# A new order for the last 138 steps of a written-out schedule: gated linear attention followed by a hard-swish feed-forward block

## The chip, the cores and the metric

The kernel runs on one core of a Trainium2 chip. The metric is the device time of one execution in microseconds (us), the median of several runs. The profile is one further execution taken by the hardware profiler; it gives every instruction's start and duration, counted from the start of the span.

Five engines work side by side, each with its own stream of instructions in a fixed order: TensorE (PE, matrix products; PEld is its weight load), VectorE (DVE), ScalarE (ACT), GpSimd (POOL) and SyncE (SP), which here issues all the transfers to and from device memory.

## The reference

Two blocks run one after the other. The first is a recurrent attention, per batch and head, over 768 time steps with a 48 x 48 state:

```python
for t in range(S):
    state = alpha[:, :, t, :, None] * state + np.einsum('bhd,bhe->bhde', k[:, :, t], v[:, :, t])
    y[:, :, t] = np.einsum('bhd,bhde->bhe', q[:, :, t], state)
```

Its output is laid out as 3072 tokens by 384 features and goes through a feed-forward block with 2048 hidden features:

```python
h = x @ w_in
g = h * np.clip(h + 3.0, 0.0, 6.0) / 6.0
return g @ w_out
```

## The kernel before, in words

**Tiling.** The attention works on chunks of 128 tokens (numbered 0 to 23, six for each of four batches). Two chunks make a group of 256 tokens (numbered 0 to 11), and the feed-forward block runs once per group. For groups from 2 on, both matrix products of that block are done by recombined blocks (fewer products, at the price of sums before and after them): sums of input blocks on VectorE, 20 products for the first matrix, seven for the second, and sums of the results.

**How the order is set.** Nothing is scheduled by a planner at build time. The kernel holds a text of 1,788 short words at the end of the main function (L763 on); `run` splits it and calls one small function for each word. A word is a step name with its numbers, such as `P.11.6` for product 6 of group 11. Within an engine, instructions run exactly in the order of the words; between engines, semaphores hold an instruction back until what it reads is written and what it overwrites has been read.

**The steps that matter here**, with the lines of the profile:

- `xc.g.i` (L537, L539; VectorE, 128x128): one of eleven sums of input blocks.
- `M.g.i` (L600; TensorE): one of 20 first products, four matmuls of 128x128; those that begin an accumulation name one of the four PSUM banks.
- `n.g.i.z` (L606; ScalarE): copies a product out of PSUM into slot z, one of sixteen areas of 128x512.
- `o.g.o.step` (L537, L539, L541; VectorE, 128x512): combines products into hidden block o (0 to 7).
- `e.g.o.z` (L494; ScalarE) and `h.g.o` (L498; VectorE): the hard-swish gate of that block; z is one of two buffers between them.
- `s.g.i` (L647, L664; VectorE): six sums of the gated hidden blocks for the second matrix.
- `P.g.i` (L703; TensorE): one of the seven second products, eight matmuls with 192 columns. The first four of them read the first half of the operand and the last four the second half.
- `K.g.i` (L682; ScalarE): keeps an intermediate result of these products.
- `G.g.i.z` (L719 on VectorE for i of 0 to 2, L716 on ScalarE for i = 3): forms one quarter of the group's output (128x192) in output buffer z, one of four; `G.g.0` follows product 1, `G.g.1` product 4, `G.g.2` product 5 and `G.g.3` product 6.
- `O.g.i` (L724; issued on SyncE): stores that quarter to device memory, 96 KB. Before buffer z is written again, its store must have landed.

Group 11 is the last one. Its seventh product, `P.11.6`, is the last work of TensorE; `G.11.3` then copies the result and `O.11.3` stores it. After the last step, SyncE waits for all stores and the engines meet in a closing exchange of semaphores (it carries line L928).

The last two lines of the text of steps, as they were:

```python
e.11.2.0 h.11.2 s.11.4 e.11.3.1 h.11.3 P.11.1.0 s.11.5 G.11.0.1 O.11.0 O.10.3 K.11.1
P.11.4 G.11.1.2 P.11.5 G.11.2.1 O.11.2 P.11.6 G.11.3.0 O.11.3 O.9.2 O.11.1
```

Of the kernel before, what the change touches and what calls it, by code (L numbers as in the profile page):

```python
# [17 lines left out]
def kernel(  # L18
# [42 lines left out]
    G = 2  # L61
# [510 lines left out]
    for i in range(8):  # L572
        r, o = divmod(i, 3)
        spots.append(raws[r].rearrange("p n w -> p (n w)").bitcast(FP)[:, o * QB : (o + 1) * QB])
    xc = consts.tile([C, len(X_SUMS), C], FP, tag="xc")
# [174 lines left out]
    with tc.manual_schedule():  # L750
# [133 lines left out]
               M.10.12 M.10.5 e.10.1.0 sv.23.1 n.10.12.13 qa.23.0 n.10.5.15 o.10.3.0 M.10.6.1  # L884
               o.10.3.1 M.10.13 n.10.13.13 o.10.2.0 e.10.3.1 M.10.18.3 n.10.18.13 o.10.2.1 o.10.6.0
               ya.22.1 yb.22 ya.23.2 yb.23 cy.23 M.10.15.0 M.10.16 M.10.14 M.10.19 cy.22 o.10.7.0
               h.10.1 xc.11.1 xc.11.3 o.10.4.0 xc.11.0 M.10.17 xc.11.4 o.10.6.1 xc.11.5 xc.11.6
               e.10.2.0 h.10.2 M.11.0.1 xc.11.2 P.10.0.2 xc.11.8 o.10.7.1 n.11.0.13 e.10.7.0 xc.11.7
               M.11.7.0 o.10.5.0 h.10.3 xc.11.9 h.10.7 e.10.6.1 e.10.5.0 h.10.5 M.11.1 K.10.0
               n.11.7.14 n.11.1.9 e.10.4.0 P.10.1.3 O.9.0 M.11.8 M.11.2 n.11.2.15 h.10.4 h.10.6  # L890
               G.10.0.2 s.10.0.10 xc.11.10 s.10.2.8 s.10.1.12 P.10.3.3 K.10.2 s.10.3.11 s.10.5
               s.10.4 M.11.3 M.11.4 n.11.4.10 P.10.2 o.11.0.0 e.11.0.0 M.11.9 o.11.1.0 M.11.5 K.10.1
               P.10.4 G.10.1.0 O.10.1 h.11.0 e.11.1.1 h.11.1 n.11.5.12 M.11.10 M.11.15.1 n.11.10.8
               P.10.5 G.10.2.0 O.10.2 O.9.1 O.10.0 M.11.11 n.11.11.11 M.11.16 o.11.4.0 M.11.18.3
               n.11.18.10 o.11.7.0 o.11.6.0 M.11.12 n.11.12.15 o.11.3.0 M.11.17 M.11.19 o.11.5.0
               M.11.13 o.11.7.1 e.11.4.0 h.11.4 n.11.13.10 o.11.2.0 e.11.7.1 P.10.6 h.11.7 G.10.3.0
               M.11.14 o.11.6.1 e.11.5.0 e.11.6.1 M.11.6.3 P.11.0.1 h.11.5 h.11.6 s.11.0.15
               s.11.1.14 s.11.3.10 P.11.3.2 K.11.0 s.11.2.11 o.11.2.1 o.11.3.1 P.11.2 K.11.2
               e.11.2.0 h.11.2 s.11.4 e.11.3.1 h.11.3 P.11.1.0 s.11.5 G.11.0.1 O.11.0 O.10.3 K.11.1
               P.11.4 G.11.1.2 P.11.5 G.11.2.1 O.11.2 P.11.6 G.11.3.0 O.11.3 O.9.2 O.11.1""")  # L900


# [30 lines left out]
```

## Time and profile before

| what | value |
|---|---|
| median of 3 runs | 536.4 us (536.31 to 536.47) |
| the profiled execution's own time | 536.33 us |
| its span, first to last instruction | 534.5 us |
| TensorE busy | 524.2 us, 98% |
| VectorE busy | 477.1 us, 89% |
| ScalarE busy | 257.6 us, 48% |
| GpSimd busy | 50.4 us, 9% |
| transfers | 43.0% of 16 engines' span |
| granted TensorE clock | full, in all 40 slices |

The time of the profiled execution is 1.8 us above its span: that lies around the instructions, outside what the profile shows. A busy share is an average over the whole span; what a changed order does has to be read where it stands, in the last eighth of the span and in what comes after TensorE's last product.

### The profile page before, as it was taken

The page shows a single profiled execution, that of the slowest core. Times are in us where ns is not written, and L with a number is a line of the kernel's source. Part 1 is how long each engine was busy: PE and PEld are TensorE (multiplying, and loading weights), DVE is VectorE, ACT ScalarE, POOL GpSimd, SP SyncE. Part 2 cuts the span into 40 slices and gives each one's busy share as a digit, 9 for nine tenths or more (in the row PEclk, how much of TensorE's full clock was granted, in tenths as well). Part 3 has the DMA queues.
Part 4 walks back from the last instruction along what each step waited for, and adds up shares of the span by engine and source line. Part 5 has one row for each costly group of instructions (what it writes and reads, how often), then busy time and mean ns, then how long its engine had stood idle before and what let it go on. Part 6 is the DMA issues. An engine that isn't in the chain of part 4 may idle for free.

```text
span 534.5 us, 15145 instructions
## 1 busy us (share of the span) xinstructions
PE 524.2 (98%) x6306; PEld 498.9 (93%) x6306; DVE 477.1 (89%) x849; ACT 257.6 (48%) x503; POOL 50.4 (9%) x71
## 2 busy tenths in 40 slices
PE   7799999999999999999999999999999999999997
PEld 7698886789999999999999999999999999999996
DVE  6999989999999899998999999999999898586381
ACT  3889864212653553543644434642633544553330
POOL 5333435100000000000010000000000000000000
PEclk9999999999999999999999999999999999999999
DMA  9998877006615155254354455055364042100001
GB/s 174 215 255 256 208 220 164 7 2 158 149 32 121 28 132 130 50 136 101 82 109 113 95 124 139 20 129 122 81 144 97 18 97 48 36 3 1 29 1 44
DMA packets 124100, 54.40 MB, mean 102 GB/s; under 512 B 83328, under 2 KB 116864, under 8 KB 124032
## 3 DMA queue, kind: packets, MB, share of 16 engines
q1 hardware_dynamic: 124032, 53.44, 43.0%
q8 instruction: 49, 0.80, 0.7%
q14 instruction: 19, 0.16, 0.1%
HBM read 44.50 MB, written 8.91 MB: 100 GB/s over the span
## 4 chain that ended last, share of the span: by engine, by line
PE 88%; DVE 6%; POOL 2%; ACT 1%; DMA 1%; issue 0%; SPq 0%; DVEq 0%; POOLq 0%
PE m_ps L703 34%; PE m_ps L600 34%; PE m_ps L478 6%; PE t_ps L455 4%; PE t_ps L346 2%; PE t_ps L429 2%; PE m_ps L489 2%; DMA v<-in_v_dram 1%; PE m_ps L516 1%; DVE rings L647 1%; PE t_ps L282 1%; DVE raw L537 1%; ACT raw L191 1%; DVE g_sb L647 1%; DVE w L537 1%; POOL v L96 1%
## 5 line engine op out<-in xcount | busy, mean ns | idle before, releaser
L606 ACT COPY g_sb<-m_ps 128x512 f32<-128x512 f32 x110 | 63.7, 584 | 124.1 <-PE m_ps L600 101.3
L703 PE MATMUL m_ps<-w,g_sb 128*128 128x192 f32 x704 | 121.7, 327 | 0.0
L703 PEld LDWEIGHTS m_ps<-w,g_sb 128*128 128x128 f32 x704 | 113.7, 190 | 0.4
L703 PE MATMUL m_ps<-rings,g_sb 128*128 128x192 f32 x528 | 91.5, 326 | 0.0
L703 PEld LDWEIGHTS m_ps<-rings,g_sb 128*128 128x128 f32 x528 | 85.4, 190 | 0.1
L600 PE MATMUL m_ps<-xc,w 128*128 128x128 f32 x640 | 82.7, 277 | 0.3 <-DVE w L541 0.3
L600 PEld LDWEIGHTS m_ps<-xc,w 128*128 128x128 f32 x640 | 77.5, 192 | 1.5 <-issue 0.5
L494 ACT ACTIVATE r<-g_sb,half 128x512 f32<-128x512 f32 x80 | 57.0, 722 | 31.5 <-DVE g_sb L541 12.4
L498 DVE SCALAR_TENSOR_TENSOR g_sb<-r,g_sb 128x512 f32<-128x512 f32 x80 | 53.7, 682 | 6.8 <-ACT r L494 5.4
L600 PE MATMUL m_ps<-xT,raw 128*128 128x128 f32 x400 | 52.5, 277 | 0.0
L600 PEld LDWEIGHTS m_ps<-xT,raw 128*128 128x128 f32 x400 | 48.6, 192 | 0.6
L409 POOL TENSOR_TENSOR st<-sm,R 128x192 f32<-128x192 f32 x20 | 12.9, 643 | 353.7 <-DVE sm L439 295.7
L647 DVE TENSOR_TENSOR g_sb<-g_sb 128x512 f32<-128x512 f32 (+1 forms) x55 | 42.1, 793 | 1.3 <-PE m_ps L703 1.1
L600 PE MATMUL m_ps<-xT,w 128*128 128x128 f32 x320 | 42.0, 276 | 0.0
L600 PEld LDWEIGHTS m_ps<-xT,w 128*128 128x128 f32 x320 | 39.3, 192 | 0.1
L366 ACT COPY A<-q 48x256 f32<-48x256 f32 x88 | 35.5, 404 | 5.0 <-DVE q L332 3.7
L356 DVE TENSOR_TENSOR A<-t_ps,mask 64x256 f32<-64x256 f32 x96 | 36.0, 413 | 0.4
L478 PE MATMUL m_ps<-xT,w 128*128 128x256 f32 x144 | 32.8, 382 | 0.0
L600 PE MATMUL m_ps<-xc,raw 128*128 128x128 f32 x240 | 31.8, 276 | 0.0
L478 PEld LDWEIGHTS m_ps<-xT,w 128*128 128x128 f32 x144 | 26.7, 190 | 3.6
L309 DVE TENSOR_TENSOR_SCAN R<-t,ones 128x516 f32<-128x516 f32 x24 | 29.6, 1233 | 0.5 <-ACT t L300 0.4
L600 PEld LDWEIGHTS m_ps<-xc,raw 128*128 128x128 f32 x240 | 29.6, 192 | 0.1
(104 smaller groups left out, 730.3 us busy)
## 6 DMA issues: line engine op xcount, KB each, us to landing
raw<-in_moe_w_out_dram SPq DMA_DIRECT2D x8, 768.0 KB, 5.3
raw<-in_moe_w_in_dram SPq DMA_DIRECT2D x6, 768.0 KB, 7.1
v<-in_v_dram SPq DMA_DIRECT2D x48, 96.0 KB, 3.0
out_dram<-oh SPq DMA_DIRECT2D x44, 96.0 KB, 1.7
far<-kq SPq DMA_DIRECT2D x64, 64.0 KB, 2.2
kb<-far SPq DMA_DIRECT2D x64, 64.0 KB, 2.1
aq<-in_alpha_dram SPq DMA_DIRECT2D x36, 96.0 KB, 2.4
qq<-in_q_dram SPq DMA_DIRECT2D x36, 96.0 KB, 2.5
```

The lines of the kernel that those rows point to most:

```text
L309: nc.vector.tensor_tensor_scan(out=reverse(R, n - 1, n), data0=reverse(ax, n, n), data1=reverse(ones, n, n), initial=0.0, op0=ALU.mult, op ...
L356: nc.vector.tensor_tensor(out=to[:, a], in0=sc[a][half], in1=mask[half, half].unsqueeze(1).to_broadcast([HB, NP, HB]), op=ALU.mult)
L366: nc.scalar.copy(out=to[:, a], in_=Q_t[j][64 * a : 64 * a + D, :, half])
L409: nc.gpsimd.tensor_tensor(out=st, in0=sm, in1=R_t[j][:, :, 0:1].to_broadcast([C, NP, D]), op=ALU.mult)
L455: nc.tensor.matmul(y_of(j, (i + 1) // 2, p)[:, HB * b : HB * b + HB], vb[:, p, e : e + 32], A_t[j][:, b, 2 * p + a], start=(b == 0 and i = ...
L478: nc.tensor.matmul(h[:, f], w1[:, kk, o : o + C], xT_t[g][:, kk], start=(kk == 0), stop=(kk == KT - 1))
L494: nc.scalar.activation(out=to, in_=h, func=AF.Relu, bias=half, scale=1.0 / 6.0)
L498: nc.vector.scalar_tensor_tensor(out=to, in0=r, scalar=1.0, in1=h, op0=ALU.min, op1=ALU.mult)
L600: nc.tensor.matmul(acc[g][i][:, f * C : (f + 1) * C], spots[w][:, f * C : (f + 1) * C], x_of(g, x), start=(first and f == 0), stop=last, s ...
L606: nc.scalar.copy(out=slots[z], in_=acc[g][i])
L647: nc.vector.tensor_tensor(out=out, in0=in0, in1=in1, op=ALU.subtract)
L703: nc.tensor.matmul(to[g], a, rhs[:, f], start=(first and f == 0), stop=(last and f == HF - 1), skip_group_check=True)
```

## The change

The first 1,650 words of the step text stay as they are. The last 138 words, from 471.8 us of the span on, hold the same steps in another order, and in some of them another slot or buffer number. No step is added or taken away.

On TensorE two pairs of products are exchanged: `M.11.1` now stands ahead of `M.11.7`, and `M.11.15` ahead of `M.11.10`; every other product keeps its place. On VectorE and ScalarE many sums, gates and copies change places. On SyncE the last eleven stores change places; on GpSimd nothing changes. The output buffers of four steps differ: `G.10.1` from 0 to 1, `G.11.0` from 1 to 2, `G.11.1` from 2 to 0 and `G.11.3` from 0 to 2.

The last stores stand in these orders:

```
before: O.9.0  O.10.1 O.10.2 O.9.1 O.10.0 O.11.0 O.10.3 O.11.2 O.11.3 O.9.2 O.11.1
after:  O.9.1  O.9.0  O.10.2 O.10.0 O.10.3 O.10.1 O.11.0 O.11.2 O.11.1 O.9.2 O.11.3
```

The diff:

```diff
@@ -884,20 +884,20 @@
                M.10.12 M.10.5 e.10.1.0 sv.23.1 n.10.12.13 qa.23.0 n.10.5.15 o.10.3.0 M.10.6.1
                o.10.3.1 M.10.13 n.10.13.13 o.10.2.0 e.10.3.1 M.10.18.3 n.10.18.13 o.10.2.1 o.10.6.0
                ya.22.1 yb.22 ya.23.2 yb.23 cy.23 M.10.15.0 M.10.16 M.10.14 M.10.19 cy.22 o.10.7.0
-               h.10.1 xc.11.1 xc.11.3 o.10.4.0 xc.11.0 M.10.17 xc.11.4 o.10.6.1 xc.11.5 xc.11.6
-               e.10.2.0 h.10.2 M.11.0.1 xc.11.2 P.10.0.2 xc.11.8 o.10.7.1 n.11.0.13 e.10.7.0 xc.11.7
-               M.11.7.0 o.10.5.0 h.10.3 xc.11.9 h.10.7 e.10.6.1 e.10.5.0 h.10.5 M.11.1 K.10.0
-               n.11.7.14 n.11.1.9 e.10.4.0 P.10.1.3 O.9.0 M.11.8 M.11.2 n.11.2.15 h.10.4 h.10.6
-               G.10.0.2 s.10.0.10 xc.11.10 s.10.2.8 s.10.1.12 P.10.3.3 K.10.2 s.10.3.11 s.10.5
-               s.10.4 M.11.3 M.11.4 n.11.4.10 P.10.2 o.11.0.0 e.11.0.0 M.11.9 o.11.1.0 M.11.5 K.10.1
-               P.10.4 G.10.1.0 O.10.1 h.11.0 e.11.1.1 h.11.1 n.11.5.12 M.11.10 M.11.15.1 n.11.10.8
-               P.10.5 G.10.2.0 O.10.2 O.9.1 O.10.0 M.11.11 n.11.11.11 M.11.16 o.11.4.0 M.11.18.3
-               n.11.18.10 o.11.7.0 o.11.6.0 M.11.12 n.11.12.15 o.11.3.0 M.11.17 M.11.19 o.11.5.0
-               M.11.13 o.11.7.1 e.11.4.0 h.11.4 n.11.13.10 o.11.2.0 e.11.7.1 P.10.6 h.11.7 G.10.3.0
-               M.11.14 o.11.6.1 e.11.5.0 e.11.6.1 M.11.6.3 P.11.0.1 h.11.5 h.11.6 s.11.0.15
-               s.11.1.14 s.11.3.10 P.11.3.2 K.11.0 s.11.2.11 o.11.2.1 o.11.3.1 P.11.2 K.11.2
-               e.11.2.0 h.11.2 s.11.4 e.11.3.1 h.11.3 P.11.1.0 s.11.5 G.11.0.1 O.11.0 O.10.3 K.11.1
-               P.11.4 G.11.1.2 P.11.5 G.11.2.1 O.11.2 P.11.6 G.11.3.0 O.11.3 O.9.2 O.11.1""")
+               O.9.1 h.10.1 xc.11.0 xc.11.1 xc.11.3 o.10.4.0 M.10.17 o.10.6.1 xc.11.4 xc.11.5
+               xc.11.2 xc.11.6 xc.11.8 e.10.2.0 h.10.2 M.11.0.1 P.10.0.2 o.10.7.1 n.11.0.13 M.11.1
+               xc.11.7 M.11.7.0 xc.11.9 o.10.5.0 e.10.7.0 h.10.7 h.10.3 e.10.5.0 h.10.5 s.10.1.14
+               e.10.6.1 K.10.0 e.10.4.0 P.10.1.3 O.9.0 n.11.7.9 M.11.8 n.11.1.10 M.11.2 h.10.4
+               h.10.6 G.10.0.2 xc.11.10 s.10.0.15 P.10.3.3 s.10.2.12 s.10.3.8 s.10.5 s.10.4
+               n.11.2.11 M.11.3 M.11.4 P.10.2 n.11.4.14 o.11.0.0 M.11.9 o.11.1.0 K.10.1 K.10.2
+               e.11.0.0 e.11.1.1 M.11.5 n.11.5.15 P.10.4 G.10.1.1 h.11.0 h.11.1 M.11.15.1 M.11.10
+               P.10.5 G.10.2.0 O.10.2 O.10.0 n.11.10.8 M.11.11 n.11.11.12 M.11.16 o.11.4.0 M.11.18.3
+               n.11.18.14 o.11.7.0 M.11.12 n.11.12.11 o.11.6.0 o.11.3.0 M.11.17 M.11.19 o.11.5.0
+               e.11.5.0 M.11.13 o.11.7.1 e.11.4.1 h.11.4 n.11.13.14 o.11.2.0 e.11.7.1 P.10.6 h.11.7
+               G.10.3.0 O.10.3 O.10.1 M.11.14 o.11.6.1 M.11.6.3 P.11.0.1 h.11.5 e.11.6.1 h.11.6
+               s.11.0.11 s.11.1.8 s.11.3.9 P.11.3.2 K.11.0 s.11.2.14 P.11.2 o.11.3.1 K.11.2 o.11.2.1
+               e.11.2.0 h.11.2 s.11.4 e.11.3.1 h.11.3 P.11.1.0 G.11.0.2 s.11.5 O.11.0 K.11.1 P.11.4
+               G.11.1.0 P.11.5 G.11.2.1 O.11.2 P.11.6 G.11.3.2 O.11.1 O.9.2 O.11.3""")
 
 
 # ---- launch: one core; float64 goes in as its bits, since the chip has no such type ----
```

## The prediction, made before the changed kernel had run

> **What bounds the kernel now.** I read the page's busy shares first, then the stretches at the end of the span, then the chain that ended last, then SyncE's own queue and its waits.
>
> ```profile
> PE 524.2 (98%) x6306; PEld 498.9 (93%) x6306; DVE 477.1 (89%) x849; ACT 257.6 (48%) x503; POOL 50.4 (9%) x71
> ```
>
> TensorE is busy for 98%. The changed steps begin at 471.8 us, so the share has to be read from there on. The next view gives the busy time of each engine by stretch (length first, then PE, PEld, DVE, ACT, POOL, clock, transfer share and GB/s):
>
> ```profile
> 470.00:490.00 20.00, 20.00 (x269) 19.91 (x261) 17.04 (x34) 8.30 (x15) 0.00 (x0) 1.00 0.01 2
> 490.00:510.00 20.00, 20.00 (x154) 20.00 (x153) 8.38 (x14) 7.00 (x12) 0.00 (x0) 1.00 0.07 21
> 510.00:530.73 20.73, 20.73 (x133) 20.43 (x131) 11.25 (x18) 3.85 (x8) 0.00 (x0) 1.00 0.04 14
> 530.73:534.50 3.77, 0.00 (x0) 0.00 (x0) 0.00 (x0) 0.32 (x1) 0.00 (x0) 1.00 0.24 78
> ```
>
> TensorE has no gap from 470 to 530.73 us, at the full clock; 3.77 us follow in which it does nothing. A reordering that keeps all products can't shorten the first part; it can only put gaps into it. The second part can shrink. The chain says the same, in order of time (start, length, what):
>
> ```profile
> 512.53 18.22 PE m_ps L703 x112
> 530.74 0.02 issue
> 530.77 0.32 ACT oh L716
> ```
>
> The last seven second products run back to back, ScalarE copies the last quarter, and then come the stores. SyncE's queue, one instruction at a time:
>
> ```profile
> 531.11 0.33 SPq L724 DMA_DIRECT2D out_dram<-oh  x1
> 531.50 0.42 SPq L724 DMA_DIRECT2D out_dram<-oh  x1
> 531.97 0.43 SPq L724 DMA_DIRECT2D out_dram<-oh  x1
> ```
>
> By the order of the words these three are O.11.3, O.9.2 and O.11.1. Only the first is of data just made. `G.11.1` ended at 525.92 us (525.57 plus 0.36, VectorE's row of L719), and `G.9.2` some 70 us earlier; both stores stand behind O.11.3 and wait with it. SyncE's waits in the last 10 us (in total, times, longest):
>
> ```profile
> SPq L724 <- DVE oh L719: 3.8, 1, 3.8
> SPq L724 <- ACT oh L716: 2.1, 1, 2.1
> SPq L928 <- DMA out_dram<-oh: 1.1, 3, 0.4
> ```
>
> The 2.1 us is O.11.3's wait for the ScalarE copy, with the two finished quarters queued behind it; the last line is SyncE waiting three times for a landing at the close. The tail cut at the transfers' own marks:
>
> ```profile
> 530.74:531.94 1.20, 0.00 (x0) 0.00 (x0) 0.00 (x0) 0.32 (x1) 0.00 (x0) 1.00 0.00 1
> 531.94:532.42 0.48, 0.00 (x0) 0.00 (x0) 0.00 (x0) 0.00 (x0) 0.00 (x0) 1.00 0.64 205
> 532.42:532.91 0.49, 0.00 (x0) 0.00 (x0) 0.00 (x0) 0.00 (x0) 0.00 (x0) 1.00 0.63 202
> 532.91:533.39 0.48, 0.00 (x0) 0.00 (x0) 0.00 (x0) 0.00 (x0) 0.00 (x0) 1.00 0.63 202
> 533.39:534.52 1.13, 0.00 (x0) 0.00 (x0) 0.00 (x0) 0.00 (x0) 0.00 (x0) 1.00 0.00 0
> ```
>
> 205 GB/s over 0.48 us is 98 KB, one store. So the three pass one after another, and the trace's records of their landing are at 532.72, 533.20 and 533.69 us. From the last landing to the end of the span are 0.83 us of closing exchange.
>
> **What the Trainium skill says.** "DMA: Bandwidth & Descriptors", section "Anatomy of one DMA — SWDGE (gpsimd) path", puts a fixed cost of about 2.0 us on a transfer, most of it the confirmation that the last byte has landed, with the moving of bytes on top. Here the stores go out from SyncE, not GpSimd, and O.11.3 took 1.61 us from issue to landing, data included; the trace's number is used. The same page, "Queues, rings and completion order", says that completion is not first in, first out per issuing engine, though each ring is consumed in order. Here the three landed in the order of issue, 0.48 and 0.49 us apart. "Perfetto Trace Analysis", section "Tensor Engine Instruction (MATMUL, LD_WEIGHTS)", says that TensorE's end times are estimates; here the copy starts 0.04 us after the modelled end of the last product, so they hold well enough.
>
> **The change part by part.**
>
> *1. The last stores.* Before, SyncE's last entries are O.11.2, O.11.3, O.9.2, O.11.1; now O.11.2, O.11.1, O.9.2, O.11.3. O.11.2 goes out at 528.61 us as before, when `G.11.2` is done (528.58). Each issue behind another takes about 0.43 us on SyncE. O.11.1 then goes out at about 529.0 and O.9.2 at about 529.5 us, both with data long ready; SyncE is free again at 529.9, 1.2 us before O.11.3's copy ends at 531.09. O.11.3 goes out at 531.11, alone and last. O.9.2, the nearest ahead of it, has landed by about 529.5 + 1.7 = 531.2, before O.11.3's bytes start to move at 531.94, so nothing shares the way. O.11.3 lands at 532.72, as it did. The last landing comes 533.69 - 532.72 = 0.97 us sooner. It consists of two issues, 531.97 - 531.11 = 0.86, and of 0.11 by which the third store took longer to land (1.72 against 1.61). SyncE's other waits at the close (some 0.06 us each) start at 531.44 and are through before 532.72. The closing 0.83 us stays.
>
> *2. The earlier stores.* O.9.1 goes out some 41 us sooner, behind O.9.3 at 461.4; nothing is queued there. O.10.1 is now behind O.10.3 and waits with it for `G.10.3` (511.10) instead of going out at 497.9. Queued behind them is only O.11.0, whose quarter is ready at 523.3. No other transfer is issued after 456 us, so no load is held up. The buffers: `G.10.1` takes buffer 1 (O.9.1 landed near 463); `G.11.0` buffer 2 (O.10.0 out at 502.7, landed 504.4; written at 522.97); `G.11.1` buffer 0 (O.10.3 out 511.1, landed 512.8; written 525.57); `G.11.2` buffer 1 (O.10.1 out 511.5, landed 513.2; written 528.2); `G.11.3` buffer 2 (O.11.0 out 523.35, landed 525.0; written 530.77). The thinnest of these leaves 5.8 us. Cost: nothing, covered by those intervals.
>
> *3. The sums and gates in front of TensorE.* Here a gap could arise. I stepped through the new order with the rows' own durations and starting distances (128x512 on VectorE: 0.69 us long, 0.60 from start to start; 128x128: 0.29 and 0.20; gate 0.72 and 0.63; copy from PSUM 0.58 and 0.49; an M every 0.89, half a P every 1.30; 0.04 us from one engine to another). The old order stepped through in this way gives every product's start within 0.03 us of the trace, so the method can be trusted for the new. The covers that come out, as the time between the last needed operand and the product's start in the old timing:
>
> - `M.11.0` at 476.30 needs `xc.11.5`. VectorE now waits for `M.10.14` (ends 474.68) with `o.10.6.1` from 474.72, then `xc.11.4` at 475.32 and `xc.11.5` from 475.55 to 475.84. Cover 0.46, was 0.50.
> - `P.10.3` at 485.96 needs `s.10.0`. It comes after `G.10.0` (484.38, held by the end of `P.10.1`) and now also after `xc.11.10`, 0.20 us more: done 485.54 instead of 485.34. Cover 0.42, was 0.62. Its second half needs `s.10.1`, which moved up by 5 us.
> - `M.11.15` now starts at 497.34 instead of 498.23, and its bank must have been read by `n.11.5` (done 495.97). Cover 1.37.
> - `M.11.14` at 510.58 needs the bank that `n.11.13` reads. That copy now stands behind two gates and ends at 509.83 instead of 508.81. Cover 0.75, was 1.77.
> - `P.11.3` at 514.97 needs `s.11.0` (514.63): cover 0.34, unchanged. The second half of `P.11.1` at 521.47 needs `h.11.3` (521.17): cover 0.30, unchanged.
> - `P.11.5` at 525.37 needs `s.11.5`, which now runs after `G.11.0` (522.97), its first half from 523.25 to 523.94. Cover 1.4, was 3.0. In exchange O.11.0 leaves 0.6 us sooner.
> - `K.10.2` moved down from 488.77 to 493.4; `P.10.5` needs its bank at 499.12. Cover 5.
>
> No cover is used up, so each of these edits costs nothing while TensorE's own work hides it. The exchanged pairs of M steps have the same size. Cost between -0.05 and +0.1 us in all.
>
> *Sum.* 534.52 - 0.97 + 0 = 533.55 us of span. The profiled execution had 536.33 with its 534.5, so 535.36 in its terms; it lies 0.07 below the median of 536.4, so 535.4 as a median. That is 0.18% less.
>
> **The rivals.**
>
> *The last store isn't what ends it: within 0.2%, at 536.2 to 536.5.* If a landing took its time from something other than its place in the queue, a lone last store would land as late as the third did. Against it: O.11.2, alone at 528.61, landed at 530.23, again 1.6 us. For it speaks only that the closing part isn't broken down by the page. A milder form, in which SyncE's remaining waits follow the last landing instead of preceding it, costs at most three of 0.06, about 0.2 us: 535.6.
>
> *TensorE waits for a sum: slower.* The place is `P.10.3`, the thinnest cover that the change makes thinner by a noticeable amount. `s.10.0` would have to be 0.42 late before anything is lost, 1.39 late to eat the whole gain, and 0.42 + 0.97 + 1.07 = 2.5 us late for 0.2% slower: 537.5 us and up. VectorE has 1.5 us of idle time just ahead of `G.10.0` and everything that `s.10.0` reads is done by 482.9, so this needs four unforeseen VectorE operations of 0.60 in that place. The same for the other thin covers.
>
> *More than the sum: faster by over 0.2%.* It needs 1.07 us, 0.10 beyond the estimate. The spread of the three runs is 0.16 us, and the closing exchange may vary by as much.
>
> **How the numbers follow.** 0.2% is 1.07 us, about what a measurement of this kernel can tell from no change, and the likeliest case lies just inside it. Likeliest case with its scatter: 0.84 (its own range 535.1 to 535.7); of this I put 0.32 beyond the 1.07 us and 0.52 within. No gain from the order of stores: 0.08, of which 0.06 within and 0.02 slower, should the runs of the two kernels differ by a shift of their own. A new wait on TensorE: 0.08, of which 0.06 ends slower and 0.02 within. In all faster 0.32, same 0.60, slower 0.08. The range from 535.1 to 536.1 holds the likeliest case and partly eaten gains and leaves out most of the two rivals, some 0.15.
>
> **What would show it.** Right: TensorE still ends near 530.7 with no gap after 470; SyncE shows issues at 528.6, 529.0, 529.5 and one alone at 531.1; after it there is one stretch of 0.48 us of transfer, and the span ends near 533.55. Wrong: an idle time of TensorE at one of the products named in part 3 (the sums), a store that waits for a buffer, or a last landing later than 1.7 us after the last issue (part 1).

## The result and the profile after

The changed kernel takes 535.5 us (median of 20 runs, 535.17 to 536.78) where the kernel before takes 536.57 (20 runs, 536.21 to 537.98). The ratio is 0.9982, with a 95% interval from 0.9975 to 0.9988: 0.18% faster. (The two medians by themselves stand 1.07 us apart, 0.20%.) The profiled span is 533.65 us instead of 534.52.

The busy times by stretch, with the last two cut at TensorE's last end (length, then PE, PEld, DVE, ACT, POOL, clock, transfer share, GB/s):

```profile
470.00:490.00 20.00, 20.00 (x269) 19.91 (x270) 17.28 (x34) 7.92 (x14) 0.00 (x0) 1.00 0.01 2
490.00:510.00 20.00, 20.00 (x154) 20.00 (x153) 7.70 (x13) 7.08 (x13) 0.00 (x0) 1.00 0.04 11
510.00:530.82 20.82, 20.82 (x134) 20.53 (x132) 11.93 (x20) 3.91 (x8) 0.00 (x0) 1.00 0.09 28
530.82:533.66 2.84, 0.00 (x1) 0.00 (x0) 0.00 (x0) 0.32 (x1) 0.00 (x0) 1.00 0.12 37
```

TensorE still has no gap from 470 us to its end. That end is 0.09 us later than before, and the 0.09 is there already at 471.8 us, where the changed words begin; every TensorE start from there on, slot for slot, is late by the same 0.09. So the new order costs TensorE nothing. The part without TensorE is 2.83 us instead of 3.79 (to the end of the span, from the instructions' own times).

The chain that ended last goes the same way as before:

```profile
512.62 18.22 PE m_ps L703 x112
530.84 0.02 issue
530.86 0.32 ACT oh L716
```

What differs is SyncE's queue, one issue at a time (by the order of the words O.11.2, O.11.1, O.9.2 and O.11.3):

```profile
528.70 0.33 SPq L724 DMA_DIRECT2D out_dram<-oh  x1
529.09 0.42 SPq L724 DMA_DIRECT2D out_dram<-oh  x1
529.56 0.43 SPq L724 DMA_DIRECT2D out_dram<-oh  x1
531.20 0.33 SPq L724 DMA_DIRECT2D out_dram<-oh  x1
```

O.11.2, O.11.1 and O.9.2 go out while TensorE works on its last product; the store of the last-made quarter is alone. SyncE's waits in the last 9 us (total, times, longest; two lines of the view) say it from the other side:

```profile
SPq L724 <- ACT oh L716: 1.1, 1, 1.1
SPq L928 <- DMA out_dram<-oh: 1.0, 1, 1.0
```

The wait for the ScalarE copy fell from 2.1 to 1.1 us, since SyncE had stores to issue meanwhile, and it waits for one landing at the close instead of three. The tail in stretches has one transfer left, but for the last bytes of O.9.2 in its first 0.1 us:

```profile
530.82:532.03 1.21, 0.00 (x1) 0.00 (x0) 0.00 (x0) 0.32 (x1) 0.00 (x0) 1.00 0.02 6
532.03:532.51 0.48, 0.00 (x0) 0.00 (x0) 0.00 (x0) 0.00 (x0) 0.00 (x0) 1.00 0.63 205
532.51:533.66 1.15, 0.00 (x0) 0.00 (x0) 0.00 (x0) 0.00 (x0) 0.00 (x0) 1.00 0.00 0
```

The last landing is at 532.82, 1.62 us after the issue, and 0.83 us before the end, the same closing time as before.

### The profile page after: what moved, and what is told of

Same layout as the page of the kernel before. It is cut to its first block, busy times and chain, and to the rows that moved or that the text cites. A ratio compares the mean times of both kernels' runs of the same rounds, so it can differ in the third digit from the quotient of the medians.

```text
span 533.7 us, 15143 instructions
## 1 busy us (share of the span) xinstructions
PE 524.6 (98%) x6306; PEld 499.4 (94%) x6306; DVE 477.2 (89%) x849; ACT 257.2 (48%) x503; POOL 50.4 (9%) x71
## 4 chain that ended last, share of the span: by engine, by line
PE 85%; DVE 8%; POOL 2%; DMA 2%; ACT 1%; issue 1%; SPq 1%; DVEq 0%; POOLq 0%
PE m_ps L703 34%; PE m_ps L600 34%; PE m_ps L478 5%; PE t_ps L455 4%; PE t_ps L346 2%; PE t_ps L429 2%; PE m_ps L489 2%; PE t_ps L282 1%; DVE rings L647 1%; DMA v<-in_v_dram 1%; DVE raw L537 1%; ACT raw L191 1%; DMA kq<-in_k_dram 1%; DVE g_sb L647 1%; DVE w L537 1%
## 5 line engine op out<-in xcount | busy, mean ns | idle before, releaser
L703 PE MATMUL m_ps<-w,g_sb 128*128 128x192 f32 x704 | 121.7, 327 | 0.0
L703 PEld LDWEIGHTS m_ps<-w,g_sb 128*128 128x128 f32 x704 | 113.7, 190 | 0.4
L703 PE MATMUL m_ps<-rings,g_sb 128*128 128x192 f32 x528 | 91.5, 326 | 0.0
L703 PEld LDWEIGHTS m_ps<-rings,g_sb 128*128 128x128 f32 x528 | 85.4, 190 | 0.1
```

What stands on the lines that cost most here:

```text
L703: nc.tensor.matmul(to[g], a, rhs[:, f], start=(first and f == 0), stop=(last and f == HF - 1), skip_group_check=True)
```

## The experiments

In all of them "tail" is the time from TensorE's last end to the end of the span. In what follows the ratio is to the kernel before, run on the same chip in the same session.

**Which part brings the gain.** The first two experiments take the change apart: the last three stores alone, and everything but them.

```diff
 the kernel before
-P.11.6 G.11.3.0 O.11.3 O.9.2 O.11.1
+P.11.6 G.11.3.0 O.11.1 O.9.2 O.11.3
```

> The kernel before with one edit: the last three stores in the order O.11.1, O.9.2, O.11.3 instead of O.11.3, O.9.2, O.11.1; all other steps in the old order. If the whole gain is in the tail: from TensorE's last end to the end of the span 2.8 us instead of 3.8, span 0.9 to 1.0 us below that of before, ratio near 0.998. If the reordered sums and gates bring the gain: no change, ratio 1.000 within 0.0005, tail 3.8 us.

Measured: ratio 0.998 (0.9971 to 0.9989), 535.67 us against 536.58, both medians. The stretch after TensorE's last end:

```profile
531.36:534.19 2.83, 0.00 (x1) 0.00 (x0) 0.00 (x0) 0.32 (x1) 0.00 (x0) 1.00 0.12 37
```

The tail is that of the changed kernel, to within 0.01 us. The span of this one profiled execution, 534.19, is only 0.33 us below that of before; TensorE's end is 0.63 us later in it, and 0.74 us are there already at 94 us, long before the edit (see the last section). The runs and the tail agree on the gain.

```diff
 the changed kernel
-P.11.6 G.11.3.2 O.11.1 O.9.2 O.11.3
+P.11.6 G.11.3.2 O.11.3 O.9.2 O.11.1
```

> The changed kernel with one edit: its last three stores put back to O.11.3, O.9.2, O.11.1; all other changed steps stay. If the whole gain is in the tail: the gain is gone, ratio 1.000 to the kernel before within 0.0005, tail 3.8 us, TensorE without a gap from 472 us on. If the reordered sums, gates and earlier stores bring something of their own: ratio clearly off 1.000 (0.998 if all of it).

Measured: ratio 1.0001 (0.9993 to 1.001). The last two stretches:

```profile
510.00:531.25 21.25, 21.25 (x136) 20.95 (x134) 12.35 (x20) 4.24 (x9) 0.00 (x0) 1.00 0.06 19
531.25:535.04 3.79, 0.00 (x1) 0.00 (x0) 0.00 (x0) 0.32 (x1) 0.00 (x0) 1.00 0.25 78
```

The gain is gone, the tail is 3.79 us again, and TensorE has no gap. Three words of the 138 carry the result. The reordered sums, gates, copies and earlier stores together are worth nothing that can be measured: the interval leaves them at most some 0.5 us either way, and in the traces TensorE takes 436.57 us here from the start of its first second product to its end, and 436.60 in the kernel before.

**What one store behind the last costs.** Two more points on the same line: one store behind the last-made one, and three.

```diff
 the changed kernel, one behind
-P.11.6 G.11.3.2 O.11.1 O.9.2 O.11.3
+P.11.6 G.11.3.2 O.9.2 O.11.3 O.11.1
 the changed kernel, three behind
-G.11.2.1 O.11.2 P.11.6 G.11.3.2 O.11.1 O.9.2 O.11.3
+G.11.2.1 P.11.6 G.11.3.2 O.11.3 O.9.2 O.11.1 O.11.2
```

> The changed kernel with one of the two stores moved back: O.9.2, O.11.3, O.11.1. If every store behind the last-made one costs one issue and one transfer in line: tail 2.83 + 0.48 = 3.3 us, half of the gain left, ratio near 0.999. If only the last of three is slow, or if the first store behind is hidden in the landing of O.11.3: tail 2.8 us and ratio 0.998.

> The changed kernel with three stores behind the last-made one: O.11.3, O.9.2, O.11.1, O.11.2. If each costs one place in line: tail 2.83 + 3 x 0.48 = 4.3 us, that is 0.5 us slower than the kernel before, ratio near 1.001. If the cost saturates because transfers overlap: tail 3.8 us or less, ratio 1.000 or below.

Measured: one behind gives 0.9988 (0.998 to 0.9996) and this tail:

```profile
531.59:534.90 3.31, 0.00 (x1) 0.00 (x0) 0.00 (x0) 0.32 (x1) 0.00 (x0) 0.91 0.19 59
```

Three behind give 1.0008 (1.0 to 1.0016) and this one:

```profile
531.81:536.09 4.28, 0.00 (x0) 0.00 (x0) 0.00 (x0) 0.32 (x1) 0.00 (x0) 0.87 0.29 92
```

With 0, 1, 2 and 3 stores behind, the tail is 2.83, 3.31, 3.79 and 4.28 us: 0.48 or 0.49 each, with no sign of saturation. (The clock column reads 0.91 and 0.87 in these two stretches; TensorE has no product in them, and the steps stay the same.) The landings of stores queued behind one another stand 0.47 to 0.50 us apart in all of these runs, which is also how long one 96 KB store moves, and they move without a pause between them. The prediction split the same 0.97 us into 0.86 of issue and 0.11 of longer landing; the simpler reading is one place in line at 0.48.

**How much cover the new order leaves.** The prediction rests on `P.10.3` having its operand 0.42 us early. Repeats of the sum `xc.11.10`, which write the same values again, were put ahead of `s.10.0` on VectorE.

```diff
 the changed kernel (four more; eight more in the second)
-G.10.0.2 xc.11.10 s.10.0.15
+G.10.0.2 xc.11.10 xc.11.10 xc.11.10 xc.11.10 xc.11.10 s.10.0.15
```

> The changed kernel with xc.11.10 done five times instead of once ahead of s.10.0 (same values each time), to measure the cover of P.10.3. If the cover is the 0.43 us that the trace of the changed kernel shows: s.10.0 is done 4 x 0.20 to 0.24 = 0.8 to 0.95 us later, TensorE idles 0.4 to 0.5 us at P.10.3 and ends that much later, ratio to before near 0.999. If the order of the sums has much more room than stepped through: no idle time, ratio 0.998.

> The same with nine instead of one: s.10.0 1.6 to 1.9 us later, idle time of TensorE at P.10.3 1.2 to 1.5 us, none of it won back later because TensorE has no slack to the end; ratio to before 1.0005 to 1.001. If the delay were absorbed later, the end would move by less than the idle time.

For comparison, `s.10.0` and `P.10.3` in the changed kernel (start, length, what; the view ends before the product does, so its length is cut):

```profile
484.95 0.68 DVE L664 TENSOR_TENSOR g_sb<-g_sb 128x512 f32<-128x512 f32 x1
486.06 1.47 PE L703 MATMUL m_ps<-w,g_sb 128*128 128x192 f32 x8
```

Measured with four more (in brackets the idle time before it, with what ended it):

```profile
484.50 1.59 DVE L537 TENSOR_TENSOR xc<-xT,xc 128x128 f32<-128x128 f32 x5
...
486.00 0.68 DVE L664 TENSOR_TENSOR g_sb<-g_sb 128x512 f32<-128x512 f32 x1
...
486.74 2.54 PE L703 MATMUL m_ps<-w,g_sb 128*128 128x192 f32 x14 [0.77 <-DVE g_sb L664]
```

and with eight more:

```profile
485.44 2.89 DVE L537 TENSOR_TENSOR xc<-xT,xc 128x128 f32<-128x128 f32 x9
...
488.25 0.69 DVE L664 TENSOR_TENSOR g_sb<-g_sb 128x512 f32<-128x512 f32 x1
...
488.99 2.22 PE L703 MATMUL m_ps<-w,g_sb 128*128 128x192 f32 x12 [2.08 <-DVE g_sb L664]
```

An added sum costs 0.33 us, not the 0.20 to 0.24 that was expected, so the idle times (0.77 and 2.08 us) and both ratios came out above what was expected. Counted from the start of `M.11.2`, the product ahead (485.16 us in the changed kernel, 484.91 and 485.85 here), `s.10.0` is done 0.47 us later in the changed kernel, 1.77 and 3.09 in these: it is late by 1.30 and 2.62 us. `P.10.3` starts 0.90, 1.83 and 3.14 us after the same mark: 0.93 and 2.24 late. So the cover is 1.30 - 0.93 = 0.37 and 2.62 - 2.24 = 0.38 us: the 0.43 us between operand and start in the trace, less some 0.05 for handing over. From the start of the first second product of the program to that of the last, TensorE takes 1.03 and 2.28 us more than in the changed kernel: what is lost at `P.10.3` reaches the end in full (the further 0.10 and 0.04 lie within the 0.11 by which this time differs between the other traces). The ratio with four more is 1.0001 (0.9992 to 1.0009), that is, the whole gain eaten, as -0.96 + 1.03 says. With eight more it is 1.005 (1.0037 to 1.0064), over the 1.0025 that -0.96 + 2.28 gives; it rests on four runs, and in the profiled one the first second product starts 0.8 us later than in the changed kernel, ahead of the edit. The rest of that difference stays open.

**Can the last store itself be made shorter?** What remains of the tail is 0.32 us of copy, 1.62 us from issue to landing, 0.83 us of closing and 0.06 us of handing over. Of the 1.62 us, 0.83 pass before the first byte moves (531.20 to 532.03), 0.48 while the bytes move and 0.31 from there to the landing. Four kernels try to shorten the copy and the store, or ask why a try failed. (`C` is 128 rows and `HB` is 64.)

```diff
 store2, for the last quarter of the last group alone
-nc.sync.dma_start(out=to, in_=o)
+nc.sync.dma_start(out=to[0:HB], in_=o[0:HB])
+nc.scalar.dma_start(out=to[HB:C], in_=o[HB:C])
```

> The changed kernel with the very last store split by rows: 64 rows issued on SyncE and 64 on ScalarE, 48 KB each. If the 0.48 us of moving one store is set by what one queue can feed: both halves move side by side, the last landing comes 0.15 to 0.25 us sooner, tail 2.6 us instead of 2.83. If it is set by the writing, or the second queue is slower at its first use: tail 2.8 us or longer.

Measured: a tail 0.60 us longer than that of the changed kernel. The ratio, 0.9991 (0.9983 to 0.9999), is 0.0009 above that of the changed kernel, with intervals that overlap, so the reading rests on the tail:

```profile
530.83:534.26 3.43, 0.00 (x0) 0.00 (x0) 0.00 (x0) 0.32 (x1) 0.00 (x0) 0.81 0.13 31
```

Both issues took longer than that of a whole store (0.55 on SyncE and 0.58 on ScalarE instead of 0.33) and the halves landed 1.9 and 2.2 us after their issue began. The next kernel splits the copy as well:

```diff
 output2, for the last quarter of the last group alone, and the split store
-nc.scalar.copy(out=o, in_=at_t[g, 6])
+nc.scalar.copy(out=o[:, 0:h], in_=at_t[g, 6][:, 0:h])
+nc.vector.tensor_copy(out=o[:, h:HD], in_=at_t[g, 6][:, h:HD])
```

> As e7, and the last copy is split too: 96 columns on ScalarE, 96 on VectorE, both out of the same PSUM bank. A copy of 192 columns takes 0.32 us there; half of it, with a fixed part, some 0.2. If the two engines read side by side: 0.1 us sooner than e7, tail 2.5 us. If they hold each other up in the bank, or the meeting of both ends costs a further semaphore: as e7 or longer.

Measured: ratio 1.0002 (0.9993 to 1.001), tail 3.63 us. The two copies didn't run side by side:

```profile
531.73 0.24 ACT L720 COPY oh<-m_ps 128x96 f32<-128x96 f32 x1 [10.08 <-PE m_ps L703]
532.00 0.26 DVE L721 COPY oh<-m_ps 128x96 f32<-128x96 f32 x1 [2.46 <-ACT oh L720]
```

By this trace VectorE waited for ScalarE's copy, so the two were put in order by the program, and the experiment doesn't tell whether the bank would have let both read at once. The last two ask which half of e7 made it slow, the second queue or the split by rows:

```diff
 the whole last store on the other queue
+nc.scalar.dma_start(out=to, in_=o)
 both halves on one queue
+nc.sync.dma_start(out=to[0:HB], in_=o[0:HB])
+nc.sync.dma_start(out=to[HB:C], in_=o[HB:C])
```

> The changed kernel with the whole last store issued by ScalarE, which also makes the copy, instead of SyncE. If the split store of e7 was slow because of the second queue: issue or landing longer than 0.33 and 1.61 us here too, tail 3.0 us or more. If the queue isn't to blame: issue 0.33, landing 1.6, tail 2.8 us (at best 0.03 less, the step from ScalarE to SyncE).

> The changed kernel with the last store split into two of 64 rows, both on SyncE. If the split by rows is what made e7 slow: each issue 0.55 us here too, and the second behind the first, tail 3.3 us or more. If the side by side of two queues made it slow: issues of 0.33 and 0.43 us, and half the bytes each, tail 2.83 + 0.2 to 0.4 us.

Measured on the other queue: tail 2.87 us, 0.04 longer than in the changed kernel, and ratio 0.9984 (0.9976 to 0.9993), no different from it. Its issue:

```profile
531.91 0.38 ACTq L729 DMA_DIRECT2D out_dram<-oh  x1
```

In halves on one queue: tail 3.91 us, ratio 0.9997 (0.9988 to 1.0006). Their issues, and the transfers from the first issue to the end of the first half's bytes:

```profile
531.25 0.55 SPq L729 DMA_DIRECT2D out_dram<-oh  x1
531.84 0.60 SPq L730 DMA_DIRECT2D out_dram<-oh  x1
```

```profile
531.25:532.45 1.20, 0.00 (x0) 0.00 (x0) 0.00 (x0) 0.00 (x0) 0.00 (x0) 1.00 0.00 0
532.45:532.87 0.42, 0.00 (x0) 0.00 (x0) 0.00 (x0) 0.00 (x0) 0.00 (x0) 1.00 0.52 117
```

The queue is not to blame; the split is. A store of 64 rows takes longer to issue than one of 128 rows (0.55 against 0.33 us) and longer to land (1.93 us for the first of these, 1.62 for the whole). Both parts of that can be seen: its first byte moves 1.20 us after the issue began, where that of a whole store took 0.83, and its half of the bytes takes 0.42 us instead of 0.48, at 117 GB/s instead of 205. Why 64 rows cost that, the runs don't show; a split by columns was not tried. The second half landed 0.66 us after the first, with a pause of 0.22 us between their bytes. So the 0.48 us for one place in line holds for whole stores of 96 KB and did not shrink with the bytes here. None of the four beats the changed kernel.

## Why the prediction was right

The time was 535.5 us where 535.4 was forecast, the ratio 0.9982 where 0.18% less was. Both medians of 20 runs lie 0.1 to 0.2 us above what the forecast, made from three runs, started from and came to; that the absolute time fits so closely is in part luck, the difference is not.

*Part 1, the last stores: right, mechanism and size.* The tail shrank by 3.79 - 2.83 = 0.96 us; 0.97 was worked out. The issues were expected at 528.6, 529.0, 529.5 and 531.1 and came at 528.70, 529.09, 529.56 and 531.20, all with the 0.09 us that this execution brought along. The lone last store landed after 1.62 us (1.61 forecast). e1 and e2 show that this part is the whole of it, and e3 and e4 that it goes on in the same steps. One reading in this part was off: `G.9.2` ended at 466.07 us (465.72 plus 0.35), 60 us and not 70 before `G.11.1`; its data was long ready all the same.

*Part 2, the earlier stores: right.* No copy waited for a buffer; O.10.3 and O.10.1 went out at 511.22 and 511.59, O.11.0 at 523.45 (forecast 511.1, 511.5 and 523.35). e2 holds them all and is no slower than the kernel before.

*Part 3, the sums in front of TensorE: right in the result, one size off.* The covers in the trace of the changed kernel against those stepped through: `P.10.3` 0.43 (0.42), `M.11.15` 1.37 (1.37), `M.11.14` 0.76 (0.75), `P.11.3` 0.33 (0.34). `M.11.0` is the exception, 0.37 instead of 0.46. The term at fault is the time from one 128x128 sum to the next, 0.20 us in the rule of the prediction and 0.23 in its list (475.32 to 475.55); in the trace `xc.11.5` follows `xc.11.4` by 0.32 (475.41 to 475.73). 0.20 holds when the second doesn't read the first; `xc.11.5` reads `xc.11.4`. The trace of before had such pairs (`xc.11.1` to `xc.11.3`, 473.03 to 473.35, is 0.32), and e5 shows 0.33 for sums that write the same place. It did no harm here because 0.37 us were still cover. The room ahead of `P.10.3` was also a little smaller than worked out: what `s.10.0` reads was done at 483.12 us (482.9 was forecast; 0.09 of the difference is this execution's own), and VectorE then idled for 1.36 us (1.5).

*The rivals.* That the last store doesn't end the kernel is refuted by the four evenly spaced tails, and its milder form by the closing time, 0.83 us before and after. The wait of TensorE at `P.10.3` didn't come; e5 and e6 show that the mechanism is real, with a threshold of about 0.37 us (0.42 was argued), and that beyond it the loss reaches the end undiminished. The chance of 0.60 for "within 0.2%" fell to the right side, but that is luck: 0.18% is just inside, and the interval from 0.12 to 0.25% reaches over the line. The scatter was put too small as well: the three runs of before spread over 0.16 us, all 20 over 1.77, and the 20 of the changed kernel over 1.61.

## What to carry to other kernels

When the bound engine has no gap to its end, read what follows its last instruction as a stage of its own: every store issued behind the one of the last-made data cost a place in line here (0.48 us for 96 KB), and a store whose data is ready belongs in front of the one that has to wait. A change of order that keeps the bound engine's work can be judged by the cover of each operand, stepped through with durations from the trace, but with two spacings, one for independent and one for dependent neighbours (here 0.20 and 0.32 us). Splitting a last store isn't a safe way to shorten it; in halves by rows it took longer.

## What the runs showed that was not expected

- In the twelve profiled executions (before, after and the experiments) nearly all of the spread ahead of the tail is there by some 94 us. The first of the second products (L703) starts between 93.99 and 95.25 us, 1.26 us apart. From there to the start of the last product the time is 433.73 to 433.84 us in all but e5 and e6, which made TensorE wait at `P.10.3`. What makes the early spread was not looked into. So a gain of 1 us at the end is better read from the tail of one trace than from a single span.
- Half a store by rows (64 x 192) took 0.55 to 0.60 us to issue, where a whole one of 128 rows took 0.33 to 0.43. Its first byte moved 1.20 us after the issue began instead of 0.83, and it landed up to 0.6 us later.
- Two VectorE sums of 128x128 start 0.20 us apart when independent and 0.32 to 0.33 apart when the second reads what the first wrote, or writes the same place.
